# Re-ordering the first sequence of a fused attention and ResMLP kernel: vector rows and transposes moved, weight loads queued in another order

## The chip, the core and the metric

The kernel runs on one core of a Trainium2 chip. The metric is the device time of one execution in microseconds (us); lower is better. Engine names are those of the profile: PE (TensorE matmul), PEld (its weight loads), DVE (VectorE), ACT (ScalarE), POOL (GpSimd) and SP (SyncE, which only issues transfers). "Queue" means the list of instructions that one engine works off in order.

## The reference

Inputs are float32, and so is the output. For each of 8 sequences (B = 8, S = 384 tokens, 16 query heads, 4 key and value heads, head size 64):

```
scores = q @ k^T / 8;  attn = softmax(scores);  x = attn @ v      # x: 384 x 1024
a1  = alpha1 * x + beta1
u   = x + lam * (w_tok @ a1)                   # w_tok: 384 x 384, mixes tokens
a2  = alpha2 * u + beta2
out = u + lam * (relu(a2 @ w_ch1) @ w_ch2)     # w_ch1: 1024 x 4096, w_ch2: 4096 x 1024
```

## The kernel before, in words

All matmuls take bf16 operands and accumulate in float32, but for a few float32 ones in the first sequence. Per sequence there are two kinds of work. `main(b)` is the channel MLP. It first computes the hidden layer (line 408): 16 chunks of W1, each with two groups of 8 matmuls of 384 columns (385 in the first pass, whose last column carries beta2). Then it computes the second layer (line 435): two halves `dw` of the output columns, three row blocks each, 32 matmuls of 512 columns per block. `side(b)` is the attention and token mixing of sequence b: scores (line 202), exp on ACT (line 211), the product with v (`av_piece`, line 237, which ends in three DVE instructions: reciprocal, scaling, and the product with alpha1*lam, called g1), `tok` (line 259, and one DVE addition at line 266), and a transpose of the result into `a2T`, which main(b) reads.

The order of instructions is written by hand and kept on every engine. While main(b) runs, the small steps of side(b+1) are strewn between its matmuls, so PE stays busy. Only side(0) has nothing to hide in: it runs by itself ahead of main(0). The table `at` in `side` says which steps stand after which of the 18 groups of scores. Its names are: `k_transpose`, `q_transpose`, `wtok_transpose` (PE transposes and a DVE copy out of PSUM); `scale_rows` and `split` (small DVE work on the vectors alpha1, beta1, alpha2 and lam, each kept in `rows_f` as 8 rows of 128, repeated on 32 partitions; `split` cuts a float32 row into three bf16 parts, `rows_b`); `spread_g1` and `spread` (PE matmuls that copy a row to all 128 partitions, in float32 or from the bf16 parts, and a copy into `vecs`); `rows_r` and `fill_h` (the two small operands R and H, with which `tok` adds beta1's share in the first sequence); `ut` (`a2_transpose` in float32, scaled by `al2T` on ACT); `warmup` (matmuls on zeros that nothing reads); and `h_part` (the first two chunks of main(0), begun early).

PSUM buffers are few: scores have two, tags "tp" and "av" one each, and "mm" two, which `av`, `tok`, `warmup` and main share. A step therefore waits until the buffer's last user has copied its data out.

Loads go through three queues. SP issues k, v of sequence 0 and the rows; ACT issues q's first four heads; POOL issues everything that is converted to bf16 on the way (the rest of q, w_tok, W1, W2). W1 has a ring of five chunk buffers (`RING`), so chunk n+5 is asked for when chunk n has been used. W2 stays resident; its first half `dw` = 0 is asked for in one transfer of half its rows (`load_w2(0, 0, 2)`), and the rest in pieces behind the W1 chunks:

```
            load_w1(b * NCH + c + RING)
            if b == 0 and 2 <= c < 12:
                load_w2(*((0, 6 + c, 16) if c < 10 else (1, c - 10, 16)))
            if b == 0 and c == 12:
                for i in range(1, 8):
                    load_w2(1, i, 8)
```

`pe_flip = b < 2` chooses PE transposes for `a2T` of sequence 1 (lines 288 and 291); sequences 2 to 7 use DMA transposes from SP (line 282).

Of the kernel before, what the change touches and what calls it, by code (L numbers as in the profile page):

```python
# [12 lines left out]
def kernel(  # L13
# [21 lines left out]
    nc = tc.nc  # L35
    f32 = mybir.dt.float32
# [3 lines left out]
    MUL = mybir.AluOpType.mult  # L40
    ADD = mybir.AluOpType.add
# [6 lines left out]
    P = 128  # L48
# [75 lines left out]
    def load_w1(n):  # L124
        if n < B * NCH:
            t = sb.tile([P, NDT, CW * P], bf, tag="w1", name="w1", bufs=RING)
            c = n % NCH
            nc.gpsimd.dma_start(out=t, in_=w1src[:, :, c * CW * P:(c + 1) * CW * P])  # L128
            w1_tiles[n] = t
# [28 lines left out]
    def side(b):  # L158
# [113 lines left out]
        def a2_transpose(p):  # L272
            if first:
                ps = psum.tile([P, NST, P], f32, tag="tp" if p % 2 else "av", name="ut", bufs=1)
                for tt in range(NST):
                    nc.tensor.matmul(out=ps[:, tt, :], lhsT=x[:, tt, cols(p)], rhs=ident_f, is_transpose=True,  # L276
                                     start=(tt == 0), stop=(tt == NST - 1), skip_group_check=True)
                nc.scalar.activation(out=a2T[:, p, :S], in_=ps.rearrange("p a b -> p (a b)"),
                                     func=mybir.ActivationFunctionType.Copy, scale=al2T[:, p:p + 1])
                return  # L280
            if not pe_flip:
                nc.sync.dma_start_transpose(
                    out=a2T[:, p, :S].rearrange("p (a s) -> p a s", a=NST),
                    in_=a2s[p].rearrange("p a d -> p (a d)"))
                return
            ps = tp_ps([P, NST, P])
            for tt in range(NST):
                nc.tensor.matmul(out=ps[:, tt, :], lhsT=a2s[p][:, tt, :], rhs=ident,
                                 is_transpose=True, start=(tt == 0), stop=(tt == NST - 1),
                                 skip_group_check=True)  # L290
            nc.scalar.copy(out=a2T[:, p, :S], in_=ps.rearrange("p a b -> p (a b)"))
# [10 lines left out]


        def rows_r(tag):
            ps = psum.tile([P, S], f32, tag=tag, name="r", bufs=1)
            for st in range(NST):
                nc.tensor.matmul(out=ps[:32], lhsT=ones, rhs=wtokT[:, st, :], start=(st == 0),
                                 stop=(st == NST - 1))
            t = hTf[:32, 10240:10240 + S]
            nc.vector.tensor_copy(out=t, in_=ps[:32])  # L310
            nc.vector.scalar_tensor_tensor(out=R[:32], in0=t, scalar=masks[2], in1=ps[:32], op0=MUL, op1=ADD)


        def spread(ps_, vs, tag, eng="DVE"):
# [3 lines left out]
            for i, p in enumerate(ps_):  # L318
# [1 line left out]
                                 rhs=rows_b[:, vs[0] * P:vs[1] * P], start=True, stop=True)  # L320
            evac(eng)(out=vecs[:, vs[0]:vs[1], ps_[0] * P:(ps_[-1] + 1) * P].rearrange("p v (n d) -> p n v d", n=n),
                      in_=ps[:, :n * w].rearrange("p (n v) d -> p n v d", n=n))


        def spread_g1(ps_, tag):
            ps = psum.tile([P, 4, P], f32, tag=tag, name="vec", bufs=1)
            for i, p in enumerate(ps_):
                nc.tensor.matmul(out=ps[:, i], lhsT=ident_f[:NP, p:p + 1].to_broadcast([NP, P]),  # L328
                                 rhs=rows_f[:NP, :P], start=True, stop=True)
            nc.vector.tensor_copy(out=g1[:, ps_[0] * P:(ps_[-1] + 1) * P], in_=ps.rearrange("p n d -> p (n d)"))  # L330

        us = []

# [38 lines left out]
        def av(p):  # L372
            av_piece(p, 0)
            av_piece(p, 1)

        ut = a2_transpose
        at = {0: [(warmup, 3)], 1: [(k_transpose, 1, 1), (scale_rows,), (split, 1, 2, 0)],
              2: [(q_transpose, 2, 2, "av"), (split, 1, 2, 1)],
              3: [(spread_g1, lower, "tp")], 4: [(wtok_transpose, 0, "av"), (av, 0), (wtok_transpose, 1, "tp")],
              5: [(wtok_transpose, 2, "av"), (fill_h, 0), (k_transpose, 2)], 6: [(av, 1), (rows_r, "av")],  # L380
              7: [(q_transpose, 4, 2)], 8: [(av, 2), (fill_h, 4)], 9: [(spread_g1, upper, "tp")], 10: [(tok, 0), (av, 3)],
              11: [(tok, 1), (q_transpose, 6, 2)], 12: [(ut, 0), (tok, 2)], 13: [(av, 4), (tok, 3)], 14: [(ut, 1), (ut, 2)],
              15: [(av, 5), (ut, 3)], 16: [(tok, 4)], 17: [(av, 6), (tok, 5)]}
        for i in range(18):
            add(scores, i)
            for f, *a in at.get(i, []):
# [10 lines left out]
    def main(b):  # L397
# [3 lines left out]
        for c in range(NCH):  # L401
            w1 = w1_tiles.pop(b * NCH + c)
            for j in range(CW):
# [14 lines left out]
                    nc.vector.tensor_scalar(out=hT[:, nt, :], in0=ps[:, :S], scalar1=c1,  # L418
                                            scalar2=0.0, op0=ADD, op1=mybir.AluOpType.max)
                yield T_H  # L420
            load_w1(b * NCH + c + RING)
            if b == 0 and 2 <= c < 12:
                load_w2(*((0, 6 + c, 16) if c < 10 else (1, c - 10, 16)))
            if b == 0 and c == 12:
                for i in range(1, 8):
                    load_w2(1, i, 8)
        for dw in range(NDW):
            cs = slice(dw * 512, (dw + 1) * 512)
            for ms in range(NST):
# [18 lines left out]
    with tc.manual_schedule(engines=order):  # L448
# [9 lines left out]
        load_k(0, [0])  # L458

        hTf = hT.rearrange("p n s -> p (n s)")  # L460
        rows_f = hTf[:32, 9216:10240].bitcast(f32)
        rows_t = hTf[:32, 10240:11264].bitcast(f32)
        rows_b = hTf[:, 11264:11776]
        stage = sb.tile([P, NST * DM], f32, tag="x", name="stage", bufs=2)
        qst, vst = (stage[:, i:i + Hkv * NST * D].rearrange("p (h st d) -> p h st d", h=Hkv, st=NST)
                    for i in (0, Hkv * NST * D))
        wtok_in = stage[:, 1536:2112].bitcast(bf).rearrange("p (tt s) -> p tt s", tt=NST)
        be2, al2T = stage[:, 2112:2120], stage[:, 2856:2864]
        ident_f = hTf[:, 11776:12032].bitcast(f32)
        R = stage[:, 2120:2312].bitcast(bf)  # L470
        H = stage[:, 2312:2824].bitcast(bf)
        ones = stage[:, 2824:2840].bitcast(bf)
# [2 lines left out]
        sel = stage[:, 2852:2856].bitcast(bf)  # L475
        for t in (stage[:, 2120:2824], rows_b, sel):
            nc.vector.memset(t, 0.0)
        nc.sync.dma_start(out=vst, in_=v[0].rearrange("h (p st) d -> p h st d", st=NST))

        for i, ap in enumerate((moe_alpha1, moe_beta1, moe_alpha2, moe_lam)):  # L480
            nc.sync.dma_start(out=rows_f[:, i * P:(i + 1) * P],
                              in_=bass.AP(tensor=ap.tensor, offset=ap.offset, ap=[[0, 4], [P, NP], [1, P]]))
        load_k(0, [2])
        with nc.allow_non_contiguous_dma(reason="one small vector, once"):
            for t, ap in ((al2T, moe_alpha2), (be2, moe_beta2)):
                nc.sync.dma_start(out=t, in_=ap.rearrange("(dt di) -> di dt", di=P))
        for h in (0, 2):
            nc.scalar.dma_start(out=qst[:, h:h + 2], in_=q[0, h:h + 2].rearrange("h (p st) d -> p h st d", st=NST))
        xs[0] = sb.tile([P, NST, DM], f32, tag="x", name="x", bufs=2)
        qgs = [qst] + [sb.tile([P, G, NST, D], bf, tag="es", name="qg", bufs=EB) for _ in range(Hkv - 1)]  # L490

# [15 lines left out]
                nc.vector.tensor_reduce(out=t[:n], in_=ident[:n, :n].rearrange("p (k c) -> p c k", c=NP), op=ADD, axis=AX)  # L507


        def scale_rows():  # L510
            r = rows_f[:, :2 * P].rearrange("p (v d) -> p v d", v=2)
            nc.vector.tensor_tensor(out=r, in0=r, in1=rows_f[:, None, 3 * P:].to_broadcast([32, 2, P]), op=MUL)


        def split(lo, hi, step=None):
# [23 lines left out]
        place_k(0, 1)  # L539
        for c in range(2, RING):  # L540
            load_w1(c)
        nc.gpsimd.tensor_copy(out=a2Ts[0][:, :, S:S + 1], in_=be2[:, :, None])

        load_k(1)
        load_q(1)
# [64 lines left out]
```

## Time and profile before

| | us |
|---|---|
| median of 9 runs (lowest to highest) | 814.93 (814.03 to 816.04) |
| the profiled execution's own time | 815.34 |
| its span (first to last instruction) | 813.3 |
| PE busy | 800.0 (98%) |
| DVE busy | 344.3 (42%) |
| ACT busy | 228.0 (28%) |
| POOL busy | 179.4 (22%) |

About 2.0 us of the profiled execution lie outside its span. The first line-408 matmul of main(0) starts 43.26 us after the span's start and the first line-435 matmul 90.50 us after it; sequence 1's line 408 starts at 140.92 us. From there each sequence takes about 97.5 us.

In the profile's answers a line gives start and duration in us, then engine, source line, operation, tiles and shape; the bracket at its end is the idle time of the engine just before and what ended it. In a table of windows each engine has its busy time and, in brackets, its number of instructions; after the engines stand the share of full speed that TensorE's clock was granted, the DMA engines' share and their GB/s. Matmuls overlap, so what a group of matmuls takes is read from start to start.

### The profile page before, as it was taken

To read this page: it belongs to the slowest core of one execution; us is meant where nothing else is said; L and a number is where in the kernel's file an instruction comes from. 1 tells how busy PE (TensorE), PEld (TensorE's weight loads), DVE (VectorE), ACT (ScalarE), POOL (GpSimd) and SP (SyncE) were. 2 spreads that over 40 slices of the span, in tenths; PEclk is the share of its full clock that TensorE was granted. 3 is DMA by queue.
4 is the path that set the end of the run, shared out by engine and by line. 5 is a ranking of instruction groups with operands and counts; after the bars stand their busy time and mean duration, and the time that the engine had idled before them with its cause. 6 is when DMAs were issued, how large, how long until landed. Compare 5 with 4: busy or idle time off the path is not lost.

```text
span 813.3 us, 14143 instructions
## 1 busy us (share of the span) xinstructions
PE 800.0 (98%) x6098; PEld 453.9 (56%) x6152; DVE 344.3 (42%) x663; ACT 228.0 (28%) x315; POOL 179.4 (22%) x234
## 2 busy tenths in 40 slices
PE   7999999999999999999999999999999999999997
PEld 4766555565556655566455654556555565556545
DVE  6655553344443444334452444424444344442122
ACT  5654330432113321233103331034211432102100
POOL 6144430224003240123301341022500321003000
PEclk9999999999999999999999999999999999999999
DMA  9999998999159992799947998499944999129611
GB/s 197 198 177 200 202 213 139 178 170 175 37 133 174 180 141 61 138 180 176 117 91 130 172 179 93 112 138 178 172 73 100 154 168 135 37 64 186 89 39 39
DMA packets 232110, 112.57 MB, mean 138 GB/s; under 512 B 81008, under 2 KB 225904, under 8 KB 232048
## 3 DMA queue, kind: packets, MB, share of 16 engines
q0 software_dynamic: 169200, 83.28, 82.1%
q1 hardware_dynamic: 62304, 28.00, 14.1%
q8 instruction: 48, 0.79, 0.4%
q10 hardware_dynamic: 544, 0.39, 0.2%
q14 instruction: 14, 0.11, 0.0%
HBM read 170.53 MB, written 12.58 MB: 225 GB/s over the span
## 4 chain that ended last, share of the span: by engine, by line
PE 94%; DVE 3%; issue 1%; DMA 1%; ACT 0%; ACTq 0%; DVEq 0%
PE ch L435 41%; PE h L408 39%; PE av L237 4%; PE sc L202 4%; PE tok L259 4%; DVE hT L418 1%; DVE x L243 1%; PE h L152 1%; DMA stage<-in_q_dram 1%; DVE a1f L250 0%; DVE a L252 0%; PE ut L276 0%; PE vec L328 0%; ACT hT L211 0%; DVE rinv L242 0%
## 5 line engine op out<-in xcount | busy, mean ns | idle before, releaser
L408 PE MATMUL h<-a2T,w 128*128 128x384 bf16 (+1 forms) x2016 | 349.7, 326 | 1.0 <-DVE hT L418 0.3
L435 PE MATMUL ch<-w,hT 128*128 128x512 bf16 (+2 forms) x1546 | 346.1, 370 | 4.4 <-issue 1.0
L408 PEld LDWEIGHTS <-w 128*128 128x128 bf16 x2016 | 189.4, 98 | 125.4 <-issue 8.7
L128 POOL DMA_DIRECT2D w<-in_moe_w_ch_dram x128 | 112.6, 880 | 545.1 <-PE h L408 502.6
L435 PEld LDWEIGHTS <-hT 128*128 128x128 bf16 x1600 | 146.1, 98 | 153.0 <-issue 5.8
L211 ACT ACTIVATE es<-sc 128x1024 bf16<-128x1024 f32 x126 | 123.4, 1021 | 283.4 <-PE sc L202 283.4
L418 DVE TENSOR_SCALAR hT<-h,bias 128x384 bf16<-128x384 f32 x128 | 79.0, 618 | 187.0 <-PE h L408 186.4
L416 ACT ACTIVATE hT<-h,bias 128x384 bf16<-128x384 f32 x128 | 74.3, 581 | 202.9 <-PE h L408 202.4
L440 DVE TENSOR_TENSOR o<-ch,vecs 128x512 f32<-128x512 f32 (+2 forms) x50 | 33.4, 667 | 91.1 <-PE ch L435 91.1
L266 DVE TENSOR_TENSOR x<-tok,x 128x384 f32<-128x384 f32 x64 | 35.6, 556 | 82.1 <-PE tok L259 78.0
L237 PEld LDWEIGHTS <-es 128*128 128x128 bf16 x1008 | 45.8, 97 | 20.5
L237 PE MATMUL av<-v,es 128*128 128x65 bf16 x1008 | 49.0, 193 | 0.0
L202 PE MATMUL sc<-qT,kT 64*128 64x384 bf16 (+2 forms) x576 | 46.1, 275 | 0.8 <-DVE qT L190 0.7
L259 PEld LDWEIGHTS <-wtokT 128*128 128x128 bf16 x576 | 38.4, 99 | 12.6 <-issue 0.8
L242 DVE RECIPROCAL rinv<-av 128x6 f32<-128x6 f32 x64 | 12.4, 193 | 71.3 <-PE av L237 71.2
L259 PE MATMUL tok<-a,wtokT 128*128 128x128 bf16 x504 | 37.3, 219 | 0.0
L243 DVE TENSOR_TENSOR x<-av,rinv 128x384 f32<-128x384 f32 x64 | 35.7, 557 | 2.3
L202 PEld LDWEIGHTS <-kT 64*128 64x128 bf16 x576 | 19.9, 94 | 28.9 <-issue 23.7
L441 DVE TENSOR_TENSOR o<-o,x 128x512 f32<-128x512 f32 (+2 forms) x50 | 34.9, 697 | 1.7
L270 DVE TENSOR_TENSOR a<-x,vecs 128x384 bf16<-128x384 f32 x56 | 31.7, 566 | 1.9
L252 DVE TENSOR_TENSOR a<-a1f,vecs 128x384 bf16<-128x384 f32 x56 | 31.2, 558 | 2.2
L250 DVE TENSOR_TENSOR a1f<-x,vecs 128x384 f32<-128x384 f32 x56 | 31.2, 558 | 1.9
(75 smaller groups left out, 206.4 us busy)
## 6 DMA issues: line engine op xcount, KB each, us to landing
w<-in_moe_w_ch_dram POOLq DMA_DIRECT2D x135, 512.0 KB, 7.5
out_dram<-o SPq DMA_DIRECT2D x47, 256.0 KB, 2.0
q_raw<-in_q_dram POOLq DMA_DIRECT2D x28, 192.0 KB, 6.7
kst<-in_k_dram SPq DMA_DIRECT2D x16, 192.0 KB, 2.7
w<-in_moe_w_ch_dram POOLq DMA_DIRECT2D x10, 256.0 KB, 11.7
w<-in_moe_w_ch_dram POOLq DMA_DIRECT2D x1, 2048.0 KB, 15.3
v<-in_v_dram POOLq DMA_DIRECT2D x21, 64.0 KB, 6.9
a2T<-a SPq DMA_TRANSPOSE x48, 3.1
```

The source lines that it names most:

```text
L128: nc.gpsimd.dma_start(out=t, in_=w1src[:, :, c * CW * P:(c + 1) * CW * P])
L202: nc.tensor.matmul(out=sc[:, hh, k % 4:k % 4 + n], lhsT=kT[r, sk, 2 * p // G, :], rhs=qT[r, p, st:st + n, :], start=True, stop=True)
L211: nc.scalar.activation(out=e, in_=sc, func=EXP, scale=scale_qk)
L237: nc.tensor.matmul(out=av[:, hh, sq, :], lhsT=ess[k // 4][:, m % 2, k % 4, :], rhs=vb[:, sk, hk, :], start=(sk == 0), stop=(sk == NST - 1))
L243: nc.vector.tensor_tensor(out=x[:, :, cols(p)].rearrange("p st (h d) -> p h st d", h=2), in0=av[:, :, :, :D], in1=rinv.to_broadcast([P, 2, ...
L259: nc.tensor.matmul(out=ps[:, tt, :], lhsT=wtokT[:, st, tt * P:(tt + 1) * P], rhs=a1s[p][:, st, :], start=(st == 0), stop=(st == NST - 1 an ...
L266: nc.vector.tensor_tensor(out=u, in0=ps, in1=u, op=ADD)
L408: nc.tensor.matmul(out=ps[:, :n], lhsT=w1[:, dt, j * P:(j + 1) * P], rhs=a2T[:, dt, :n], start=(dt == 0), stop=(dt == NDT - 1))
L416: nc.scalar.activation(out=hT[:, nt, :], in_=ps[:, :S], func=RELU, bias=c1)
L418: nc.vector.tensor_scalar(out=hT[:, nt, :], in0=ps[:, :S], scalar1=c1, scalar2=0.0, op0=ADD, op1=mybir.AluOpType.max)
L435: nc.tensor.matmul(out=ps[:, lo:hi], lhsT=hT[:, nt, ms * P:(ms + 1) * P], rhs=w2[:, nt, dw * 512 + lo:dw * 512 + hi], start=(nt == 0), sto ...
L441: nc.vector.tensor_tensor(out=o[:, lo:hi], in0=o[:, lo:hi], in1=x[:, ms, c], op=ADD)
```

## The change

1. `a2_transpose` of sequence 1 goes through DMA transposes on SP for p < 6; p = 6 and 7 stay on PE.
2. In the first pass W1's chunks 5 to 15 are queued with only four of W2's pieces between them (behind c = 3, 5, 7, 9). W2's last quarter of the first half and all of its second half follow at c = 11, and the next pass's first five W1 chunks at c = 15, behind all of W2.
3. v of sequence 0 is issued by ACT, behind q. On SP the rows of alpha1 and lam come straight after the first half of k, then the other half of k, then the rows of beta1, alpha2 and beta2.
4. g1 is spread from bf16 parts: `scale_rows` and `split` run once for alpha1 (early) and once for beta1 (later), `spread_g1` is gone, and `spread` is used in its place.
5. alpha2 and beta2 are no longer loaded element by element into columns. Two small PE transposes in `rows_r` and two DVE copies make `al2T` and the bias column of `a2T`.
6. In the order of side(0): one more `warmup` matmul after scores 3; the first spread moves from step 3 to step 4, the first AV from step 4 to step 5; `rows_r`, `fill_h`, the q transposes and the `ut` steps move by one or two steps. Regions of scratch memory shift to make room for a fifth row.

```
-            if not pe_flip:
+            if not pe_flip or p < 6:
                 nc.sync.dma_start_transpose(
...
         def rows_r(tag):
-            ps = psum.tile([P, S], f32, tag=tag, name="r", bufs=1)
+            ps = psum.tile([P, 512], f32, tag=tag, name="r", bufs=1)
...
+            turned = ps[:, S:S + 2 * NP].rearrange("p (i n) -> p i n", i=2)
+            for i, c in enumerate((2, 4)):
+                nc.tensor.matmul(out=turned[:, i], lhsT=rows_f[:NP, c * P:(c + 1) * P], rhs=ident_f[:NP, :NP],
+                                 is_transpose=True, start=True, stop=True, skip_group_check=True)
...
+            nc.vector.tensor_copy(out=al2T, in_=turned[:, 0])
+            nc.vector.tensor_copy(out=a2T[:, :, S:S + 1], in_=turned[:, 1, :, None])
...
-        at = {0: [(warmup, 3)], 1: [(k_transpose, 1, 1), (scale_rows,), (split, 1, 2, 0)],
-              2: [(q_transpose, 2, 2, "av"), (split, 1, 2, 1)],
-              3: [(spread_g1, lower, "tp")], 4: [(wtok_transpose, 0, "av"), (av, 0), (wtok_transpose, 1, "tp")],
-              5: [(wtok_transpose, 2, "av"), (fill_h, 0), (k_transpose, 2)], 6: [(av, 1), (rows_r, "av")],
-              7: [(q_transpose, 4, 2)], 8: [(av, 2), (fill_h, 4)], 9: [(spread_g1, upper, "tp")], 10: [(tok, 0), (av, 3)],
-              11: [(tok, 1), (q_transpose, 6, 2)], 12: [(ut, 0), (tok, 2)], 13: [(av, 4), (tok, 3)], 14: [(ut, 1), (ut, 2)],
-              15: [(av, 5), (ut, 3)], 16: [(tok, 4)], 17: [(av, 6), (tok, 5)]}
+        at = {0: [(warmup, 3)], 1: [(k_transpose, 1, 1), (scale_rows, 0), (split, 0, 1, 0)],
+              2: [(q_transpose, 2, 2, "av"), (split, 0, 1, 1)], 3: [(warmup, 1)],
+              4: [(spread, lower, (0, 1), "tp"), (wtok_transpose, 0, "av")], 5: [(av, 0), (wtok_transpose, 1, "tp")],
+              6: [(wtok_transpose, 2, "av"), (scale_rows, 1), (split, 1, 2), (k_transpose, 2)],
+              7: [(av, 1), (q_transpose, 4, 2, "av")], 8: [(rows_r, "tp"), (fill_h, 0)],
+              9: [(av, 2), (spread, upper, (0, 1), "av")], 10: [(q_transpose, 6, 2), (tok, 0)],
+              11: [(av, 3)], 12: [(tok, 1), (ut, 0)], 13: [(av, 4), (tok, 2)], 14: [(ut, 1), (fill_h, 4), (tok, 3)],
+              15: [(av, 5), (ut, 2)], 16: [(tok, 4), (ut, 3)], 17: [(av, 6), (tok, 5)]}
...
-            load_w1(b * NCH + c + RING)
-            if b == 0 and 2 <= c < 12:
-                load_w2(*((0, 6 + c, 16) if c < 10 else (1, c - 10, 16)))
-            if b == 0 and c == 12:
-                for i in range(1, 8):
+            if b or c + RING < NCH:
+                load_w1(b * NCH + c + RING)
+            if b == 0 and c in (3, 5, 7, 9):
+                load_w2(0, 8 + c // 2 - 1, 16)
+            if b == 0 and c == NCH - RING:
+                for i in (6, 7):
+                    load_w2(0, i, 8)
+                for i in range(8):
                     load_w2(1, i, 8)
+            if b == 0 and c == NCH - 1:
+                for i in range(RING):
+                    load_w1(NCH + i)
...
-        nc.sync.dma_start(out=vst, in_=v[0].rearrange("h (p st) d -> p h st d", st=NST))
-
-        for i, ap in enumerate((moe_alpha1, moe_beta1, moe_alpha2, moe_lam)):
-            nc.sync.dma_start(out=rows_f[:, i * P:(i + 1) * P], ...
+        load_row(0, moe_alpha1)
+        load_row(3, moe_lam)
         load_k(0, [2])
-        with nc.allow_non_contiguous_dma(reason="one small vector, once"):
-            for t, ap in ((al2T, moe_alpha2), (be2, moe_beta2)):
-                nc.sync.dma_start(out=t, in_=ap.rearrange("(dt di) -> di dt", di=P))
+        load_row(1, moe_beta1)
+        load_row(2, moe_alpha2)
+        load_row(4, moe_beta2, 1)
...
+        nc.scalar.dma_start(out=vst, in_=v[0].rearrange("h (p st) d -> p h st d", st=NST))
...
-        def scale_rows():
-            r = rows_f[:, :2 * P].rearrange("p (v d) -> p v d", v=2)
-            nc.vector.tensor_tensor(out=r, in0=r, in1=rows_f[:, None, 3 * P:].to_broadcast([32, 2, P]), op=MUL)
+        def scale_rows(i):
+            r = rows_f[:, i * P:(i + 1) * P]
+            nc.vector.tensor_tensor(out=r, in0=r, in1=rows_f[:, 3 * P:4 * P], op=MUL)
...
-        nc.gpsimd.tensor_copy(out=a2Ts[0][:, :, S:S + 1], in_=be2[:, :, None])
```

## The prediction, as it was put on record before the changed kernel ran

> **What bounds the kernel now.** I read the page's first section, then a table of windows, then the timeline of the first 43 us on PE and DVE, then the DMA issues.
>
> ```profile
> PE 800.0 (98%) x6098; PEld 453.9 (56%) x6152; DVE 344.3 (42%) x663; ACT 228.0 (28%) x315; POOL 179.4 (22%) x234
> ```
>
> PE is busy for 98% of the span, so only work taken off PE, or PE's idle and half-speed time, can shorten it. The windows (PE, PEld, DVE, ACT, POOL, then the granted clock) say where that time lies:
>
> ```profile
> 6.20:10.20 4.00, 3.20 (x31) 1.58 (x31) 0.91 (x2) 3.10 (x5) 2.54 (x3) 1.00 1.32 212
> 10.30:12.00 1.70, 1.19 (x10) 1.08 (x12) 1.63 (x5) 0.60 (x1) 0.48 (x2) 0.99 1.67 133
> 12.00:15.30 3.30, 3.15 (x35) 2.03 (x32) 3.00 (x9) 1.57 (x2) 3.10 (x5) 0.50 1.52 199
> 15.40:22.20 6.80, 5.92 (x86) 3.97 (x86) 6.39 (x15) 4.57 (x6) 3.95 (x6) 1.00 1.39 212
> 22.30:25.60 3.30, 3.30 (x41) 2.80 (x39) 2.09 (x5) 1.70 (x2) 1.24 (x2) 0.50 1.46 198
> 25.70:43.20 17.50, 17.48 (x232) 13.00 (x231) 10.33 (x23) 10.47 (x16) 1.30 (x2) 1.00 1.33 184
> 43.30:140.90 97.60, 96.81 (x773) 55.36 (x780) 48.42 (x101) 36.13 (x63) 34.03 (x44) 1.00 1.25 191
> ```
>
> Three things stand in it. From 10.3 to 22.2 us DVE is the full engine (11.02 of 11.8 us), and PE is not. Twice the clock is half: about 12.0 to 15.4 and 22.2 to 25.6 us. After 25.7 us PE is without a gap. What starts DVE's stretch, and how PE stands meanwhile:
>
> ```profile
> 6.24 0.52 PE L188 MATMUL tp<-hT,stage 128*128 128x128 f32 x3 [0.78 <-DMA stage<-in_q_dram]
> 10.30 0.41 DVE L512 TENSOR_TENSOR hT<-hT 32x256 f32<-32x256 f32 x1 [1.63 <-DMA hT<-in_moe_lam_dram]
> 10.81 1.12 PE L328 MATMUL vec<-hT 8*128 8x128 f32 x8 [1.30 <-issue]
> 20.09 0.39 PE L202 MATMUL sc<-qT,kT 64*128 64x384 bf16 x4 [0.69 <-DVE qT L190]
> ```
>
> DVE sat idle 1.63 us until lam's row came, because the rows stand behind v on SP's queue; the q copy that scores 4 need stood behind that. So the first 33 us are a chain q, lam's row, DVE.
>
> **Parts 3 to 6, the start.** q: its second half landed 0.78 us after PE wanted it, while v's 384 KB came on SP's queue. With v behind q on ACT, only 192 KB of k and two 16 KB rows compete at first. The transpose then waits for the buffer "tp" instead, which the k copy frees at 5.42; I take it at 5.55 instead of 6.24, so 0.65 us (0 to 0.78). The Trainium skill, "DMA: Bandwidth & Descriptors", section "Issuing engines are not separate DMA queues", speaks against this: transfers from all queues run on the same 16 engines, so another queue saves issue time alone; this term would be 0 and the total below 0.65 smaller. v itself is wanted at about 11 us and landed at 6.3; it may come 3 us later at no cost.
>
> lam: two rows stand ahead of it on SP, not five transfers, so it lands near k's 4 us. DVE's `scale_rows` then follows the k copy (8.31 + 0.36 - 0.65 = 8.0) instead of starting at 10.30.
>
> DVE's work, from `scale_rows` to the addition of `tok(0)` (line 266, 23.02): 12.72 us before, of which 0.91 idle, so 11.81 of work. Added: a second, split `scale_rows` 0.2 (the 256-column one took 0.41); five more instructions of `split`, 1.4 (the ones before took 0.25 + 0.27 + 0.41 + 0.51 + 0.14 = 1.58 from start to start, the slow pair beside POOL's k casts); two 8-column copies at 0.15, the price of a bias copy (L414), 0.3; the last q copy, now ahead of this point, 0.47. Moved behind it: the second `fill_h`, 0.60. Sum 13.6. Idle: 0.7 (0.3 to 1.4), as before less one buffer wait plus the new relay from `rows_b` over PE's spread (0.22, the price of the bf16 spread at L319) back to DVE. So 8.0 + 13.6 + 0.7 = 22.3, against 23.02: 0.7 us won, after 2.3 us of earlier start and 1.8 us of extra work.
>
> PE in that stretch has under 8 us of work in 14 us; there the saving of the bf16 spread (1.06 and 1.09 down to 0.22 each), the added `warmup` (0.59/3 = 0.2) and the two f32 transposes (0.27 at L328's 0.135) lie under DVE and cost and bring nothing. If DVE were free they would bring 1.2 us.
>
> From there on PE is bound again. `tok(1)` waits for `tok(0)`'s buffer, 22.3 + 0.56 = 22.9. Up to `av(6)` it has four `tok` at 0.75, four `ut` at 0.39, two `av` at 0.58 and five scores at 0.32: 7.3 us, plus 0 to 0.5 of buffer waits, since DVE needs 7.3 there too. So `av(6)` starts at 30.4 at full clock; before, at 33.16. That is 2.7 us. A half-clock window in it would cost up to 1.7 us, half of 3.4. In the trace such a window followed stretches in which PE was busy 80% (3.20 of 4.00) and 87% (5.92 of 6.80); the new stretch is emptier, so I expect one around 22 us again, some of it under DVE: 0.6 us off. First stage: 2.1 us (0.8 to 3.7). Behind `av(6)` the list is the same to 43.26.
>
> The Trainium skill, "TensorE: Matmul & The Clock Gate", section "What's actually happening", lets the clock fall only after a whole idle window of about 3.4 us. The idle times here were 1.30 and 0.69 us and the clock fell all the same; by the rule no half-speed window would come, and the first stage would be worth 2.7 us.
>
> **Part 1, transposes of sequence 1.** Six groups of three leave PE. One group costs its slot:
>
> ```profile
> 87.17 0.33 PE L288 MATMUL tp<-ident,a 128*128 128x128 bf16 x3
> 87.33 0.98 PE L408 MATMUL h<-a2T,w 128*128 128x385 bf16 x5
> ```
>
> That is 0.16 to 0.17 us from start to start, 6 x 0.17 = 1.0 us, all on the path. The ACT copies (6 x 0.5) lay beside PE. Added on SP: six DMA transposes, 1.2 us of issue each, 3.1 us to landing (median of 48). Behind them on SP stand the output stores and the flips of sequence 2. Each transpose's data is ready one `tok` step (6 to 8 us) before the store that follows it, so no store waits. The last of the six issues at about 123 us and `a2T` is read at 138; even the 6 us of a loaded queue leave 9. If that cover were gone, each us is one us at the pass's start. Bounds 0 to 1.0, taken 1.0.
>
> **Part 2, the loads of W1 and W2.** Does PE wait for W1 now? The last chunk of the first pass:
>
> ```profile
> 74.14 0.90 POOL L128 DMA_DIRECT2D w<-in_moe_w_ch_dram  x1 [2.84 <-PE h L408]
> w<-in_moe_w_ch_dram POOLq DMA_DIRECT2D x1, 512.0 KB, 12.9
> ```
>
> It landed at 87.01 and its first matmul is the one at 87.33 above: 0.3 us to spare (chunk 5 had 4.2). So nothing is lost now and the reorder alone brings nothing. But with main(0) 2.1 us earlier the old order would cost about 1.8 of it. New order: a 512 KB piece takes 2.65 us and a 256 KB piece 1.3 when the queue is full. Eleven chunks and four pieces are 34.4 us, with 1.1 for two loads of k and some 2 for the start, from 43: chunk 15 at about 80.5, wanted at 85.2. W2's pieces follow at c = 11: the last of `dw` = 0 at 86, wanted near 96; those of `dw` = 1 from 89 to 107, wanted from 115 on. The next W1 chunks land from 110 to 121, wanted from 138; q of sequence 2, behind them on POOL, by 126, where its flip comes at 127. POOL stands blocked on its queue from 75 to 100, and only these wait for it. Cost 0; if W1 were late, one for one.
>
> **Sum.** 815.34 - 2.1 - 1.0 = 812.2 on the profiled execution. That one lies 0.4 over the median of 9, so I say 811.9 on the medians' scale (0.1 kept for the unseen relays). A measurement tells about 0.2%, 1.6 us, from no change.
>
> **Rivals.**
> - *Full clock.* No half-speed window where PE is bound, DVE's relays at their low end: 3.7 + 1.0, giving 810.3. For: part of the idle time before it is filled. Against: 87% busy was not enough.
> - *DVE eats it.* Relays at 1.4 and half clock after 22 us: 0.8 in the first stage and 0.7 of the transposes, 813.5. For: DVE's 1.8 us more in its full stretch.
> - *Slower: beta1's row.* `scale_rows(1)` now stands in DVE's queue ahead of the k copy, `av(1)` and two q copies, reached at about 13.6. beta1 is the fifth transfer on SP. In the trace the k load issued at 4.88 landed 6.6 us later, the beta2 column 10.6. Issued at about 4, beta1 would land by 14.6 even so, a loss of 1.0. Past 18.2 the kernel is slower by more than 0.2%; at 20 it is 811.9 + 6.4 = 818.3. Against: rows behind v were there at 10.2 at the latest.
> - *The load order does nothing by itself* is held certain; it only keeps what the start wins.
>
> **How the numbers follow.** Forecast 0.58 (811.9, itself 810.9 to 813.2), full clock 0.14, DVE eats it 0.16, slower 0.12. Of the third case three quarters lie within 0.2%, the forecast's tail gives 0.03: faster 0.73, same 0.15, slower 0.12. Range 809.9 to 814.9: it leaves out most of the slower case and the ends of the others.
>
> **What would show it.** Right: DVE's first `scale_rows` near 8, `tok(0)`'s addition near 22.3, main(0)'s first line-408 matmul near 41.1, the first pass from there to sequence 1's first line-408 matmul 96.6 us instead of 97.66, no PE wait for W1. Wrong: DVE waiting for a beta row, half clock after 30 us, or PE idle before line 408 while POOL's loads are in flight.

## The result, and the profile after

The changed kernel takes 812.38 us (median of 9 runs, 811.30 to 813.24). The kernel before took 814.93 us over its 9 runs and 814.93 over the 29 runs made beside these. The ratio is 0.997, with a 95% interval from 0.9961 to 0.9978: 2.4 us faster, between 1.8 and 3.2 (2.55 between the two medians). Forecast was 811.9.

The profiled execution took 812.79 us (span 810.9), against 815.34 (813.3) before. The page's first section:

```profile
PE 795.9 (98%) x6076; PEld 450.0 (55%) x6129; DVE 345.2 (43%) x671; ACT 225.3 (28%) x309; POOL 176.6 (22%) x230
```

PE lost 4.1 us of busy time and is still busy 98% of the span. The table of windows, with the stretches of the one shown before; the last line is the first pass, which now starts and ends earlier:

```profile
6.20:10.20 4.00, 3.67 (x33) 1.57 (x33) 2.31 (x6) 3.47 (x6) 1.21 (x2) 1.00 1.29 230
10.30:12.00 1.70, 0.65 (x9) 0.46 (x7) 1.30 (x4) 1.59 (x2) 1.70 (x3) 1.00 0.96 179
12.00:15.30 3.30, 2.33 (x43) 1.59 (x40) 2.90 (x8) 2.05 (x2) 3.30 (x6) 1.00 1.31 171
15.40:22.20 6.80, 5.24 (x89) 3.61 (x87) 6.46 (x18) 4.02 (x4) 3.43 (x5) 1.00 1.40 201
22.30:25.60 3.30, 2.67 (x45) 1.85 (x42) 3.23 (x8) 2.21 (x3) 0.92 (x2) 1.00 1.46 198
25.70:41.00 15.30, 15.28 (x210) 11.63 (x211) 10.01 (x23) 8.96 (x14) 1.62 (x2) 1.00 1.45 198
41.70:138.20 96.50, 95.81 (x756) 54.29 (x762) 47.26 (x101) 33.23 (x57) 31.46 (x41) 1.00 1.33 201
```

From 12.0 to 25.6 us DVE is the full engine, and from 10.3 us on PE is emptier than before, as forecast. But the clock column reads 1.00 in every line: in this execution the two half-clock windows are gone, and no new one came. The groups of the start (L530 and L529 are `split`, L521 is `scale_rows`, L325 is `spread`):

```profile
L202 PE MATMUL sc<-qT,kT 64*128 64x384 bf16 x16 | 2.7, 327 | 1.0 <-DVE qT L190 0.9
L530 DVE SCALAR_TENSOR_TENSOR hT<-hT,stage 32x128 f32<-32x128 bf16 x4 | 1.8, 452 | 0.1
L529 DVE CAST hT<-hT 32x128 bf16<-32x128 f32 x4 | 1.7, 420 | 0.1
L521 DVE TENSOR_TENSOR hT<-hT 32x128 f32<-32x128 f32 x2 | 0.5, 270 | 0.0
L325 PE MATMUL vec<-hT,stage 128*128 128x128 bf16 x8 | 0.8, 218 | 0.9 <-DVE hT L533 0.9
```

PE's waits are now nearly all for DVE: 0.9 us for the split rows and 0.9 for a q copy; the 0.78 us for q's transfer are gone. DVE was idle for 0.0 to 0.1 us ahead of these rows: lam's row keeps nobody waiting. `split`'s casts took 420 ns on average, 294 ns before (L520 there). DVE's first `scale_rows` and its addition of `tok(0)`, then that addition in the kernel before:

```profile
8.66 0.27 DVE L521 TENSOR_TENSOR hT<-hT 32x128 f32<-32x128 f32 x1
23.60 0.55 DVE L266 TENSOR_TENSOR x<-tok,x 128x384 f32<-128x384 f32 x1
```

```profile
23.02 0.56 DVE L266 TENSOR_TENSOR x<-tok,x 128x384 f32<-128x384 f32 x1 [0.50 <-PE tok L263]
```

DVE's stretch starts 1.64 us earlier and ends 0.58 us later.

The loads, from POOL's timeline and the list of DMA issues:

```profile
72.03 0.90 POOL L128 DMA_DIRECT2D w<-in_moe_w_ch_dram  x1 [2.38 <-PE h L407]
```

```profile
w<-in_moe_w_ch_dram POOLq DMA_DIRECT2D x1, 512.0 KB, 8.7
a2T<-a SPq DMA_TRANSPOSE x54, 2.3
```

Chunk 15 (the first of the two lines is its own transfer) is asked for at 72.03 and landed at 80.77 (87.01 before); its first matmul is at 85.48, so 4.7 us are to spare instead of 0.3. The DMA transposes went from 48 to 54.

What the starts of main(0) and of the passes give (line 407 is line 408 of before):

| | before | after | difference |
|---|---|---|---|
| main(0)'s first matmul | 43.26 | 41.62 | -1.64 |
| first pass | 97.66 | 96.61 | -1.05 |
| passes 2 to 7 together | 584.66 | 584.67 | 0 |
| last pass to the end | 87.76 | 87.98 | +0.22 |

The last 0.22 us were not followed up.

### The profile page after: what moved, and what is told of

It is laid out like the page before. It is cut to its first block, busy times and chain, and to the rows that moved or that the text cites. A ratio compares the mean times of both kernels' runs of the same rounds, so it can differ in the third digit from the quotient of the medians.

```text
span 810.9 us, 14106 instructions
## 1 busy us (share of the span) xinstructions
PE 795.9 (98%) x6076; PEld 450.0 (55%) x6129; DVE 345.2 (43%) x671; ACT 225.3 (28%) x309; POOL 176.6 (22%) x230
## 4 chain that ended last, share of the span: by engine, by line
PE 92%; DVE 4%; DMA 2%; issue 1%; POOL 0%; ACT 0%; DVEq 0%; POOLq 0%
PE ch L441 41%; PE h L407 38%; PE av L237 4%; PE sc L202 4%; PE tok L259 4%; DMA w<-in_moe_w_ch_dram 1%; DVE x L243 1%; DVE hT L417 1%; PE h L152 1%; DVE a1f L250 0%; DVE a L252 0%; DMA kst<-in_k_dram 0%; PE ut L276 0%; DVE hT L530 0%; DVE hT L529 0%
## 5 line engine op out<-in xcount | busy, mean ns | idle before, releaser
L266 DVE TENSOR_TENSOR x<-tok,x 128x384 f32<-128x384 f32 x64 | 35.5, 555 | 80.5 <-PE tok L259 78.2
```

Source lines behind the costliest of these rows:

```text
L266: nc.vector.tensor_tensor(out=u, in0=ps, in1=u, op=ADD)
```

## The experiments

Ten new kernels were run, and two kernels were profiled a second time (e10, e11); times are medians, the ratio is to runs of the kernel before on the same chip. "main(0) at" and "half clock" (the stretches before 30 us) are of the profiled execution. The last column sorts all executions by the clock: each has its mean granted clock on record. In the profiles without a half-clock stretch that mean is 0.999 or 1.0; with 3.4 us of it 0.997, with 6.8 us 0.995 or 0.996, with 10.2 us 0.993. So an execution at 0.999 or more is counted as one at full clock; the column gives how many there were, and their median.

| kernel | us | ratio (95%) | main(0) at | half clock | full clock |
|---|---|---|---|---|---|
| before | 814.93 | 1 | 43.26 | 11.96 to 15.37, 22.20 to 25.61 | 34 of 84, 813.7 to 813.8 |
| changed | 812.38 | 0.997 (0.9961 to 0.9978) | 41.62 | none | 7 of 10, 812.38 |
| e1 changed, transposes on PE | 813.38 | 0.9979 (0.9971 to 0.9988) | 41.13 | none | 8 of 12, 812.99 |
| e2 changed, old load order | 813.89 | 0.9993 (0.9984 to 1.0001) | 41.11 | none | 4 of 11, 813.82 |
| e3 before + new load order | 814.20 | 0.9993 (0.9984 to 1.0001) | 42.21 | 12.50 to 19.33 | 3 of 12, 813.34 |
| e4 e3 + DMA transposes | 813.14 | 0.9981 (0.9971 to 0.9992) | 41.41 | none | 3 of 8, 812.36 |
| e5 changed, no `warmup` at step 3 | 812.55 | 0.9975 (0.9966 to 0.9984) | 42.32 | 12.96 to 19.78 | 4 of 12, 812.46 |
| e6 changed, f32 spread | 814.96 | 0.9998 (0.9985 to 1.0011) | 44.51 | 19.90 to 26.73 | 0 of 12 |
| e7 e3 + v on ACT, rows early | 816.01 | 1.0016 (1.0007 to 1.0025) | 43.89 | 11.24 to 21.48 | 0 of 11 |
| e8 changed, three copies on ACT | 812.08 | 0.9968 (0.9957 to 0.998) | 41.44 | 13.27 to 20.10 | 6 of 8, 811.94 |
| e9 changed, 16 warmups more | 814.53 | 0.9999 (0.9986 to 1.0011) | 41.56 | none | 10 of 11, 814.33 |
| e10 e6 again | 816.31, one run | | 44.41 | 20.00 to 26.83 | 0 of 1 |
| e11 changed again | 814.23, one run | | 43.08 | 12.60 to 16.02 | 0 of 1 |
| e12 e8 + e9 | 812.70 | 0.9981 (0.997 to 0.9991) | 41.56 | none | 8 of 11, 812.50 |

The kernel before has three medians at full clock, one for each chip on which it ran beside the experiments. Read by this column, and as far as medians of different chips can be set side by side, 1.3 of the 2.55 us are there between executions at full clock; the other 1.2 us are what the kernel before loses, in the median, to its half-clock stretches.

**What each part is worth (e1 to e4).** Theory: transposes 1.0, loads nothing alone but needed with an earlier start, start about 1.

e1:

```
-            if not pe_flip or p < 6:
+            if not pe_flip:
```

> The changed kernel with part 1 undone: all eight transposes of sequence 1 on PE again. Theory (PE slots): the first pass goes back from 96.61 to 97.66 us, main(0) still starts near 41.6, so 813.4 us. Rival (the transposes lay beside other work anyway, and the first pass got shorter through the load order): the pass stays near 96.6 and the time at 812.4 us.

e2 puts back the old `load_w1` and `load_w2` order in main(), e3 puts the new one into the kernel before (its first lines):

```
-            load_w1(b * NCH + c + RING)
-            if b == 0 and 2 <= c < 12:
...
+            if b or c + RING < NCH:
+                load_w1(b * NCH + c + RING)
+            if b == 0 and c in (3, 5, 7, 9):
...
```

> The changed kernel with part 2 undone: W1's chunks behind a W2 piece each, as before. Theory (W1's margin of 0.32 us is smaller than the 1.64 us by which main(0) now starts earlier): the last chunks come too late, PE waits 1.0 to 1.5 us in all before line-407 matmuls of chunks 13 to 15, the first pass takes 97.6 to 98.1 us, the time is 813.4 to 813.9 us. Rival (the order of loads is hidden either way): 812.4 us and no wait.

> The kernel before with part 2 alone, the new load order. Theory: no PE wait for W1 existed (0.32 us were left for the last chunk), so nothing is gained: 814.9 us, first pass 97.66 us, main(0) at 43.3. Its first stage is that of before, so the trace also tells whether the two half-clock stretches of before come again in another execution: if they belong to the order of work, two of 3.4 us between 10 and 26 us; if they are chance of the clock's phase, none or others. Rival: the new order costs or brings over 0.8 us in W2's half.

e4 is e3 with e1's line turned round (`p < 6` added):

> The kernel before with parts 1 and 2 alone (DMA transposes for six groups, new load order), the first stage untouched. Theory: the first pass takes 96.6 instead of 97.66 us and nothing else moves: 813.9 us, about 40% of the whole gain of 2.55. Rival: part 1 works only with the new first stage: 814.9 us.

Differences of two ratios, with their intervals added as squares:

- Transposes: changed against e1 0.7 us (±1.0), e4 against e3 1.0 (±1.1). The traces are sharper: the first pass takes 97.61 and 97.67 us with the transposes on PE (e1, e3), 96.61 and 96.67 without (changed, e4). The six slots of 0.17 us were all on the path. At full clock e4 against e3 gives the same, 812.36 against 813.34.
- Loads: alone 0.6 us (±0.7), not shown to be anything. With the new start 1.9 (±1.0) by the medians, 1.4 at full clock, 1.1 in the profiles' first pass (97.72 against 96.61 us): in e2 PE waits for chunk 15, issued at 71.95 and landed at 86.03. PE's timeline of e2:

```profile
86.08 1.48 PE L407 MATMUL h<-a2T,w 128*128 128x385 bf16 x8 [0.94 <-DMA w<-in_moe_w_ch_dram]
```

- Start: e1 against e3 1.1 us (±1.0), changed against e4 0.9 (±1.1). About 1.0 by the medians, where 2.1 was forecast. At full clock little of it is left: e4's three executions took 812.30 to 812.49 us and the changed kernel's seven 811.30 to 812.83, and e1's median lies 0.35 below e3's. So most of this 1.0 us is that more executions kept the clock: 19 of 33 with the new start (changed, e1, e2), 40 of 104 with the old one (before, e3, e4). With the same start the share went from 4 of 11 (e2) to 7 of 10 (changed), so that the new order keeps the clock more often is not shown beyond doubt. Parts 3 to 6 were not tried each by itself.

e4 surprised: expected near 813.9, its profiled execution took 812.49, no more than the changed kernel's 812.79. It has the old start, and its clock never fell. Its windows, over the two stretches that ran at 0.50 in the kernel before, and DVE's addition of `tok(0)`:

```profile
12.00:15.30 3.30, 2.33 (x40) 1.57 (x39) 3.01 (x9) 2.39 (x3) 2.81 (x5) 1.00 1.49 205
22.30:25.60 3.30, 3.30 (x60) 2.71 (x56) 2.80 (x6) 2.26 (x3) 1.21 (x2) 1.00 1.46 198
22.37 0.56 DVE L266 TENSOR_TENSOR x<-tok,x 128x384 f32<-128x384 f32 x1 [0.19 <-PE tok L263]
```

The old order does not always lose the clock, and the execution that the forecast was worked from was the longest of three profiled ones: main(0) at 43.26, 42.21 and 41.41. Four profiled executions of the new start (changed, e1, e2, e11) gave 41.62, 41.13, 41.11 and 43.08. From here on two questions were open: what makes the clock fall, and whether DVE's stretch sets the start.

**Does the extra warmup hold the clock? (e5)**

```
-              2: [(q_transpose, 2, 2, "av"), (split, 0, 1, 1)], 3: [(warmup, 1)],
+              2: [(q_transpose, 2, 2, "av"), (split, 0, 1, 1)],
```

> The changed kernel without the extra `warmup` block at step 3. In three profiled executions of the new order of the start the clock stayed full and main(0) began at 41.1 to 41.6 us; of three with the old order one did too (main(0) at 41.41), two had half-clock windows (42.21, 43.26). Theory A (when the half-clock windows come is a matter of the execution, not of PE's work in the new order): no change, 812.3 to 812.7 us, main(0) at 41.1 to 41.6. Rival B (the extra warmup keeps the clock up): a window of half clock of about 3.4 us returns between 11 and 26 us, main(0) at 42 to 43, 813.0 to 814.0 us.

Nothing in the time (0.4 us slower, ±1.0). The profile had a half-clock stretch, with main(0) at 42.32, but e8 and e11, which have the warmup, had one too: the warmup matmul does not prevent it by itself. Full clock in 4 of 12 executions without it and in 7 of 10 with it are too few to tell whether it helps.

**Is the bf16 spread worth its DVE work? (e6, e10)** alpha1's row is not split any more (steps 1 and 2); g1 is spread in f32 again (here step 4 and the matmul, the same at step 9):

```
-              4: [(spread, lower, (0, 1), "tp"), (wtok_transpose, 0, "av")], 5: [(av, 0), (wtok_transpose, 1, "tp")],
+              4: [(spread_g1, lower, "tp"), (wtok_transpose, 0, "av")], 5: [(av, 0), (wtok_transpose, 1, "tp")],
...
+                nc.tensor.matmul(out=ps[:, i], lhsT=ident_f[:NP, p:p + 1].to_broadcast([NP, P]),
+                                 rhs=rows_f[:NP, :P], start=True, stop=True)
...
```

> The changed kernel with the f32 spread of alpha1's and lam's first rows as before (8-partition f32 matmuls, no split of that row: some five small DVE instructions fewer, 1.4 us, and PE's spread longer by 0.85 us each). Theory A (DVE without idle time from 8.6 to 25 us sets the start): tok(0)'s addition at 21.3 to 22.0 us instead of 23.1 to 23.6, main(0) at 39.9 to 40.6, 811.0 to 811.6 us. Rival B (PE sets it, so the bf16 spread was worth its price): main(0) at 41.1 to 42, 812.4 to 813.2 us.

2.3 us slower (±1.3). Both theories fell in part. Five DVE instructions less brought no earlier first spread copy: it started at 11.34 us, against 11.17 in e1. DVE merely waited longer for the slow spread on PE, 1.91 us instead of 0.47. The rest is in the second profile:

> A second look at the kernel with the f32 spread (814.96 us, main(0) at 44.51, half clock from 19.9 to 26.7 us). Theory A (its loss is the half-clock stretch that falls later, where PE is bound): with another phase the stretch is elsewhere or absent, and main(0) is at 40.5 to 42; with the same phase it is at 44 to 45 again. Rival B (the f32 spread itself delays the chain): main(0) at 43 or later even without a half-clock stretch.

The windows of e10:

```profile
16.60:19.90 3.30, 1.56 (x21) 0.87 (x21) 3.16 (x9) 1.22 (x2) 2.63 (x4) 1.00 1.31 200
20.00:26.80 6.80, 6.80 (x63) 5.22 (x61) 4.19 (x11) 2.77 (x3) 1.74 (x3) 0.50 1.46 198
```

PE was busy for 1.56 of 3.3 us, and then the clock was half for 6.8 us in which PE was never idle. That costs up to 3.4 us, where a half-clock stretch at 13 us lies partly under DVE's work. The slow spread is the likely reason why it lay there: in e6 it kept PE busy for 3.25 of the 3.41 us from 9.66, and the clock held; in e5 and e8, which got the full clock at nearly the same moment (6.13 and 6.45 us against 6.25), PE was busy 1.78 and 1.71 of these 3.41 us, and the clock fell at 13 us. The 12 times of e6 fall into two groups, 812.45 to 813.05 (4) and 814.11 to 816.17 (8). The granted clock is 0.995 to 0.998 in all 12, so the groups differ in where the half-clock stretch lay, not in whether it came; the place in the first group was not seen, since both profiles are of the second. Even the first group is no faster than the changed kernel.

**Rows early without the split of `scale_rows` (e7).** In e3, v goes on ACT's queue behind q, and alpha1's and lam's rows ahead of the second k; `scale_rows` stays one instruction:

```
-        for i, ap in enumerate((moe_alpha1, moe_beta1, moe_alpha2, moe_lam)):
+        for i, ap in ((0, moe_alpha1), (3, moe_lam), (1, moe_beta1), (2, moe_alpha2)):
+            if i == 1:
+                load_k(0, [2])
...
```

> The old kernel with the new load order, v on ScalarE's queue behind q, and the rows of alpha1 and lam ahead of the second k on SyncE's; the rest of the start as before. Against the old kernel with the new load order alone (814.2 us). Theory A (DVE's stretch starts when lam's row comes, so earlier rows start it earlier): first scale_rows at 8.6 to 9.5 us instead of 10.0 to 10.3, main(0) 0.5 to 1.5 us earlier, 813.0 to 813.8 us. Rival B (the transfers share the same engines, v or beta1 is late by as much): scale_rows at 10 or later, 814.0 to 814.5 us.

1.9 us (±1.0) slower than e3. DVE's timeline:

```profile
10.38 0.41 DVE L518 TENSOR_TENSOR hT<-hT 32x256 f32<-32x256 f32 x1 [2.42 <-DMA hT<-in_moe_beta_dram]
```

beta1's row is there at about 10.4 us. One `scale_rows` for both rows then starts no earlier than before, its `split` runs beside v's cast on POOL (v landed at 9.45, in e3 at 6.18), and the clock was half for 10.2 us. None of the 11 executions was at full clock (0.993 to 0.996). How the 1.9 us divide among these was not tried. With `scale_rows` in one piece earlier rows for alpha1 and lam thus brought nothing, because beta1's row ends the wait; in the changed kernel the second half is reached at 15.12 us, 4.7 us after that row came in e7.

**Is DVE the bound? (e8)** Two q copies and the second spread's copy move to ACT:

```
-              7: [(av, 1), (q_transpose, 4, 2, "av")], 8: [(rows_r, "tp"), (fill_h, 0)],
-              9: [(av, 2), (spread, upper, (0, 1), "av")], 10: [(q_transpose, 6, 2), (tok, 0)],
+              7: [(av, 1), (q_transpose, 4, 2, "av", "ACT")], 8: [(rows_r, "tp"), (fill_h, 0)],
+              9: [(av, 2), (spread, upper, (0, 1), "av", "ACT")], 10: [(q_transpose, 6, 2, "tp", "ACT"), (tok, 0)],
```

> The changed kernel with three copies out of PSUM (two q copies, 0.54 us each, and the second spread's, 0.67 us) on ScalarE instead of VectorE. Theory A (DVE's work sets the start): tok(0)'s addition at 21.9 to 22.5 us instead of 23.1 to 23.6, main(0) 0.8 to 1.5 us earlier (39.9 to 40.6), 811.0 to 811.6 us. Rival B (ScalarE's exponentials come late by as much, or PE bounds): main(0) at 41.1 or later, 812.2 to 813 us.

No gain that can be told (0.2 us, ±1.2). tok(0)'s addition came at 23.24, not at 22.5, in a profile with half clock from 13.27 to 20.10, in which DVE waited 1.10 us for PE's `rows_r`. At half clock PE is the slower of the two there. At full clock the six executions took 811.5 to 812.5 us, neither theory's range. e12 below has the same copies and full clock in its profile: `tok(0)`'s addition at 22.93 and main(0) at 41.56. So 1.75 us less of copies on DVE is not seen to bring more than half a microsecond (in e12 the added warmups are in it too).

**Does PE's idle time let the clock fall? (e9, e11, e12)** e9 adds warmup matmuls ahead of PE's waits:

```
-              2: [(q_transpose, 2, 2, "av"), (split, 0, 1, 1)], 3: [(warmup, 1)],
+              2: [(q_transpose, 2, 2, "av"), (split, 0, 1, 1)], 3: [(warmup, 4)],
...
-              6: [(wtok_transpose, 2, "av"), (scale_rows, 1), (split, 1, 2), (k_transpose, 2)],
-              7: [(av, 1), (q_transpose, 4, 2, "av")], 8: [(rows_r, "tp"), (fill_h, 0)],
+              6: [(warmup, 5), (wtok_transpose, 2, "av"), (scale_rows, 1), (split, 1, 2), (k_transpose, 2)],
+              7: [(av, 1), (q_transpose, 4, 2, "av"), (warmup, 4)], 8: [(rows_r, "tp"), (fill_h, 0), (warmup, 4)],
```

> The changed kernel with 16 more warmup matmuls (0.16 us each, 2.6 us in all) placed ahead of PE's four longest waits on VectorE between 10 and 20 us (3 at step 3, 5 at step 6, 4 each at the ends of steps 7 and 8). The ten profiles so far have a half-clock stretch before 27 us wherever the full clock was granted at 6.45 us or earlier (6 of 6), and none where it came at 6.98 us or later (4 of 4). Theory A (PE's idle time lets the clock fall, in the executions whose phase is unlucky): no half-clock stretch whatever the phase, main(0) at 41.0 to 41.7 us, 811.6 to 812.2 us. Rival B (the added matmuls cost what they save, or the clock falls all the same): 812.4 to 813.2 us, or a half-clock stretch in the profile.

> A second look at the changed kernel, for the phase of the clock. Theory A (phase decides): if the full clock is granted at 6.5 us or earlier, a half-clock stretch of 3.4 to 6.9 us from about 13 us and main(0) at 42 to 42.5; if at 7 us or later, none, and main(0) at 41.1 to 41.6. Rival B (the order of the work decides): no half-clock stretch whatever the phase.

> The changed kernel with three PSUM copies on ScalarE and the 16 more warmup matmuls. Theory A (what the copies won was lost to a half-clock stretch from 13.3 to 20.1 us in that profile): full clock, tok(0)'s addition at 21.8 to 22.6 us, main(0) at 39.9 to 40.8, 811.0 to 811.7 us. Rival B (nothing won by either): 812.0 to 812.8 us, main(0) at 41 or later.

e11 came out as theory A said (full clock at 5.78 us, then half clock from 12.60), with main(0) at 43.08, later than said; e9 and e12 had the full clock as early and kept it. Every change of the clock in these profiles lies a whole number of 3.41 us steps after the first full clock of its execution, and that first moment differs between executions, from 4.42 to 10.69 us. So I read PE in slices of that grid. e11, then e9, each slice followed by the next:

```profile
9.20:12.59 3.39, 0.87 (x6) 0.42 (x7) 3.20 (x6) 2.40 (x3) 3.39 (x6) 1.00 1.38 208
12.61:16.01 3.40, 3.40 (x38) 2.19 (x38) 1.75 (x5) 1.02 (x1) 3.40 (x5) 0.50 1.39 190
```

```profile
11.93:15.33 3.40, 2.13 (x31) 1.46 (x26) 1.92 (x6) 1.71 (x2) 3.40 (x6) 1.00 1.17 139
15.35:18.70 3.35, 3.34 (x45) 1.99 (x43) 3.11 (x11) 1.90 (x2) 3.35 (x5) 1.00 1.29 193
```

In e11 PE was busy 26% of a slice and the next ran at half clock; in e9 the emptiest slice is 63% busy and the clock held. Eight profiles have a half-clock stretch: in seven the slice ahead of the first fall was busy 26 to 60%, in one (e3) 69%. In the six without one, the emptiest slice was busy 61 to 72%. This fits a rule by which the busy share of a slice decides, and the phase (where the grid lies) says which moments make up a slice. It is read off these profiles, and two falls do not fit it: the one after 69% and the second in the kernel before, after a slice of 80%. How long the clock stays half, one to three steps, the shares do not explain either: it stayed so after a slice of 100% in e6 and rose after one of 94% in the kernel before. Phase alone does not do it: e9 and e12 had the full clock at 5.10 and 5.61 us, earlier than six of the eight that lost it. Theory A of e9, no half clock whatever the phase, does not hold: with the 16 warmups 18 of 22 executions kept the full clock (10 of 11 in e9, 8 of 11 in e12), without them 13 of 18 (7 of 10 changed, 6 of 8 in e8), which tells no difference.

The added warmups did not make the kernel faster: e9 is 2.4 us (±1.2) slower than the changed kernel, e12 0.9 (±1.1). In e9 DVE waited 1.23 us for PE's `wtok_transpose`, which stood behind five warmups. Both profiles also show a new wait at the second pass. SP's and PE's timeline of e12:

```profile
133.85 4.13 SPq L117 DMA_TRANSPOSE qT<-q_raw  x1
...
139.60 0.61 PE L202 MATMUL sc<-qT,kT 64*128 64x384 bf16 x8 [0.63 <-DMA qT<-q_raw]
```

q of sequence 2, queued behind W1's next chunks, landed at 133.71 and its transposition on SP took 4.1 us. The same wait cost 0.4 us in e9, 0.2 in e6 and 0.7 in e10. In the changed kernel's profile q landed at 129.86 and nobody waited. Why e9's median lies 1.2 us above its profiled execution (813.31) stays open; it is not the clock, which was full in 10 of its 11. No variant is shown to beat the changed kernel.

## Why the prediction was right, and where its steps were off

The size came out 0.5 us short of the forecast: 2.55 between the medians, 3.1 forecast from the profiled execution. The transposes' 1.0 us came as said. For the start the number held better than the mechanism, and that is in part luck: earlier rows were to start DVE's stretch earlier and so end it earlier, which did not happen, and the half-clock loss that was to stay near 22 us is what went away. Term by term:

- **Transposes, 1.0: right.** 1.05 in the pass, 1.0 in e1 and e4. The cover was mis-sized: the last one was issued at 125.80 instead of 123 and landings took 7.2 to 8.5 us instead of at most 6, so 4 to 5 us were left and not 9. That was enough.
- **Loads: right for W1.** Chunk 15 landed at 80.77 (80.5 said), wanted at 85.48 (85.2); W2's pieces landed within 2 us of the times given. "Brings nothing alone" is within e3's interval. The price without it was less than the 1.8 said: 0.94 of wait in e2's trace, 1.1 in the pass.
- **q of sequence 2: the step that failed unnoticed.** Said "by 126", landed at 129.86, because the next W1 chunks came 4.8 us later than written (125.8, not 121). The cover was about 7 us before (its transposition issued from 130.13 to 133.97, the pass at 140.92) and is 3.5 now (130.53 to 134.76, the pass at 138.23). e9, e12, e6 and e10 used it up. It was costed at nothing; in the changed kernel's profile nothing was lost by it, with half of the cover.
- **q's half, 0.65: mis-sized.** It landed 0.97 earlier (5.13 for 6.10), but the first scores came 0.14 earlier (6.55 for 6.69): the six transposes after it ran from 5.06, before the first full clock at 7.10, and took 1.49 us, where three of them at full clock took 0.45 in the kernel before. e11 won 0.32. Of that landing 384 KB of v, now behind q, are the likeliest cause; v itself came 2.6 us later (8.94 for 6.30). The Trainium skill, "DMA: Bandwidth & Descriptors", section "Issuing engines are not separate DMA queues", would give 0 for another queue alone, and no run here has v on ACT's queue ahead of q to test that.
- **`scale_rows` at 8.0: 8.66** (8.27 to 8.58 in e1, e2, e11), before 10.30. Half a microsecond of q's mis-sized lead.
- **DVE's stretch, 13.6 of work and 0.7 idle: idle right (0.66), work 14.28.** Small 32-partition instructions cost up to five times as much beside POOL, shown below. "v may come 3 us later at no cost" is the term that was put at nothing here: v landed at 8.10 us in e11, 8.94 in the changed kernel and 10.44 in e1, and POOL's work behind it fell on these instructions. `tok(0)`'s addition thus came at 23.60, 23.11 and 23.09 (changed, e1, e2) against 22.3 forecast and 23.02, 23.16, 22.37 in the old order: DVE took the whole earlier start back, which the rival "DVE eats it" had said, though it put this on longer relays and the clock.
- **From there on, right in time, but compared with a slow stretch.** tok(1) to av(6): 7.3 forecast, 24.20 to 31.52 = 7.32 measured. From `tok(0)`'s addition to main(0) the new order takes 18.02 us in changed, e1 and e2 (18.01 in e11), the old one 19.04 at full clock (e4) and 20.24 in the profile that the forecast was worked from. So 1.0 of these 2.2 us is the order of work and 1.2 the second half-clock window. As I read it, the 1.0 comes from PE having done the last q transposes and av(3) (21.08 and 22.52) by the time DVE reaches that addition, so less is left behind it, where PE is bound. At full clock it does not come out at the end: e4 reaches the addition 0.7 to 1.2 us earlier, at 22.37, and main(0) at 41.41, against 41.11 to 41.62 with the new start.
- **The clock: wrong.** A half-clock window near 22 us, 0.6 us, was expected from the busy shares ahead of the old falls; in three of four profiles of the new start none came, in the fourth it came at 12.6. The shares themselves were read over the wrong stretches: 80% was taken from 6.20 to 10.20, leaving out 10.30 to 12.00, where PE was busy 1.19 of 1.70 us just ahead of the fall; in slices of the grid the two falls follow 60 and 80%. In before's own profile the second window cost 1.2 us (43.26 - 23.02 = 20.24 against 19.04), which an execution without it does not have to win back. So the forecast started from a long execution and added too large a gain. The Trainium skill, "TensorE: Matmul & The Clock Gate", section "What's actually happening", calls the windows free-running, of 3413 ns, and the same kernel run-variable; the grid and its phase here agree. Its fall after an idle window does not: PE had been busy 0.87 of 3.39 us in e11.
- **bf16 spread "costs and brings nothing": wrong.** Putting f32 back cost 2.3 us (±1.3) in e6. The spread's own time was hidden: its first copy came at 11.34 against 11.17 us. What was not counted is where the clock falls: in both profiles with the longer spread the half-clock stretch lay at 20 us, where PE is bound.
- **Slower, by beta1's row: did not happen.** The row is there at about 10.4 (e7) and is reached at 15.12.

## What to carry to other kernels

When a start is bound by two engines in turn, an earlier transfer is worth only what the engine behind it can use: here 1.6 us of earlier rows went into DVE's fuller stretch, and at full clock main(0) began no more than 0.3 us earlier than with the old start. Before working from one profile, see whether its losses (a half-clock window, a contended cast) come in every execution; here main(0) moved by 2.0 us between executions with the same start. Sorting all executions by their granted clock costs nothing and separates what the change does from what the clock does. And when a queue is reordered, follow the last thing in it as closely as the first: W1 was safe by 4.7 us, while q at the end of the queue had half of its cover left.

## What the runs showed of the hardware that was not expected

**Small DVE instructions beside POOL.** DVE's and POOL's timelines of e11, in which v came early and its cast fell on `scale_rows`:

```profile
8.27 0.84 DVE L521 TENSOR_TENSOR hT<-hT 32x128 f32<-32x128 f32 x1
9.14 0.68 DVE L529 CAST hT<-hT 32x128 bf16<-32x128 f32 x1
9.86 0.34 DVE L530 SCALAR_TENSOR_TENSOR hT<-hT,stage 32x128 f32<-32x128 bf16 x1
10.13 0.54 DVE L190 COPY qT<-tp 128x768 bf16<-128x768 bf16 x1
10.60 1.13 DVE L529 CAST hT<-hT 32x128 bf16<-32x128 f32 x1
...
8.15 0.83 POOL L545 CAST v<-stage 128x768 bf16<-128x768 f32 x1 [3.36 <-DMA stage<-in_v_dram]
8.92 1.77 POOL L128 DMA_DIRECT2D w<-in_moe_w_ch_dram  x2
10.67 0.98 POOL L101 CAST k<-kst 128x384 bf16<-128x384 f32 x2
```

In e1, where POOL was idle until 10.50, the same five took 0.27, 0.21, 0.34, 0.54 and 0.20 us. So `scale_rows`'s multiplication went from 0.27 to 0.84 and the second cast from 0.20 to 1.13, ending about where POOL's cast or issue ends, while the copy out of PSUM kept its 0.54. Not every instruction beside POOL is hit: in e11 the multiply-add at 9.86 kept its 0.34 beside a DMA issue, and in the changed kernel one at 9.21, beside v's cast (8.99 to 9.87), took 0.79. The Trainium skill, "Trainium Architecture — The Big Picture", section "What this means for kernel authors", says that VectorE and GpSimd contend for a shared pair of ports with an exclusive lock; these rows agree with that. Where v lands decides what is hit: the last row of the first `split` was ready at 12.51 us in e11 and at 10.69 in e1, although e11's `scale_rows` had started 0.31 earlier. PE stood idle meanwhile, 74% of that slice, and the clock fell: the late rows and the half clock together put tok(0)'s addition at 25.07 in e11, 23.11 in e1.

**The clock's grid**, with the numbers given at e9: steps of 3.41 us from a first moment that differs between executions, a fall after each slice with PE busy at most 60% (7 of 7), falls after 69 and 80% without an explanation, and none after other slices of 61 to 80%.
